# Second mixture of a three-stage kernel: the slices of an expert's first product packed into PSUM banks

## The chip, the cores and the metric

The kernel runs on one core of a Trainium2 chip. The metric is the device time of one execution in microseconds (us); less is better. TensorE (PE) multiplies into PSUM, VectorE (DVE) and ScalarE (ACT) read PSUM, GpSimd (POOL) issues gathers and scatters by index, SyncE (SP) issues the plain DMAs.

## What is computed

Attention, then two mixtures of experts in a row, all in float32. Cut to the second mixture, in which the change lies:

```python
def _moe2_ref(x, w_skip, w_gate, w1, w2):      # x [2304, 512], 8 experts, w1 [8, 512, 1024], w2 [8, 1024, 512]
    do_compute = x @ w_skip > 0
    xc = x[do_compute]
    e_idx = np.argmax(xc @ w_gate, axis=1)
    ...
    for e in range(E):
        mask = e_idx == e
        h = np.maximum(xc[mask] @ w1[e], 0.0)
        y[mask] = gate_w[mask, None] * (h @ w2[e])
    out[do_compute] = xc + y
```

Each token that is not skipped goes to one expert: a first product (512 to 1024 columns), relu, a second product (1024 to 512).

## The kernel before

The tokens of an expert are gathered in tiles of 128. `layer` (line 944) runs some tiles of one expert. Its first half makes the hidden values in KF = 8 slices f of 128 hidden columns: `mm1(x, f)` (line 873) takes a PSUM tile `h` of two banks from a pool of two (`ps_h`, so four of the eight banks), calls `products` (line 597) for the matmuls of this slice, and `hidden` (line 619) for its relu. After each slice it splits one eighth of the second weight (`w2split`, line 867) and lets queued side work advance by a step. Its second half, `mm2` (line 880), takes each tile's 8 x 3 matmuls of 512 columns over the slices in order.

The second product is made in three parts, from two halves of each operand: `hh` is the relu rounded to a shorter form (ACT, line 625), `hl` is the rest (DVE, line 626, reads the same PSUM slice and `hh`), `w2h` and `w2l` are the same of the weight (lines 854, 855). The three are `hh` by `w2h`, `hh` by `w2l`, `hl` by `w2h` (line 886). So a slice's PSUM bank is free again when DVE has made `hl`.

The first product has two forms. A layer of one tile is "native" (line 601): four float32 matmuls of 128 columns for each slice, two instructions each, 64 a layer, straight from the loaded weight. A layer of two tiles takes 12 split matmuls of 256 columns a slice (line 612). In both, a slice lies in the first of the two banks of its PSUM tile, and the second stays empty: one slice fills 128 or 256 of 512 columns.

The second mixture is ten layers, in this order: `p0a` and `p1a` (one tile each of the two experts that are known first), `p0b` (one tile), `p1b` (two), then `order[2]` and `order[3]` (two tiles each) and `order[4]` to `order[7]` (one each). Seven are native. Beside `p0a` and `p1a` runs the last part of the choice of experts, which those layers' loops advance (`aux2`, `tick`): `chain7` (line 1286) computes the gate of the tokens that the last expert of the first mixture wrote, with two small matmuls (`ranks`, lines 135 and 136), and scatters the result into `slots2`. `place_rest` (line 1395) then gathers the token lists (`meta`) and rows of `p0b` and `p1b` from it. Later layers gather the rows of the next layers in their first half: `r.load()` issues the gather of `meta`, and `load_ids` (line 567) turns it into indices on DVE (`tid`, line 568) behind the split of slice 5 or so, and issues the gather of the rows.

Nothing but the order of the program's text sets the order on each engine: each engine runs its instructions one after the other, and waits on semaphores of the others.

Of the kernel before, what the change touches and what calls it, by code (L numbers as in the profile page):

```python
# [8 lines left out]
F32 = mybir.dt.float32  # L9
F32R = mybir.dt.float32r  # L10
I32 = mybir.dt.int32
AF = mybir.ActivationFunctionType
OP = mybir.AluOpType
# [26 lines left out]
def attention_moe_moe(ctx, tc, qT, kT, vm, vr, tau, wgn, noise, w1a, w2a, wsg, w1b, w2b, out):  # L40
    nc = tc.nc
# [161 lines left out]
    def pool(stack, name, bufs, side="left", **kw):  # L203
        return stack.enter_context(tc.tile_pool(name=name, bufs=bufs, side=side, reuse_waits="tile", **kw))
# [392 lines left out]
    def products(x, f, ps):  # L597

        nn = x.n * 128
        parts = [(0, nn)] if nn <= 512 else [(0, nn // 2), (nn // 2, nn // 2)]  # L600
        if x.native:
            for kd in range(KD):
                nc.tensor.matmul(ps[:, 0, 0:nn], x.raw[0, f // 4][:, kd, (f % 4) * 128:(f % 4 + 1) * 128], x.xf[:, kd],
                                 start=(kd == 0), stop=(kd == KD - 1))
                if x.fine and kd == 1:
                    yield
        else:
            wh, wl = x.s1[f]
            for kd in range(KD):
                for j, (w, v) in enumerate(((wh, x.xh), (wh, x.xl), (wl, x.xh))):  # L610
                    for c, (a, m) in enumerate(parts):
                        nc.tensor.matmul(ps[:, c, 0:m], w[:, kd, :], v[:, kd, a:a + m],  # L612
                                         start=(kd == 0 and j == 0), stop=(kd == KD - 1 and j == 2))
                if kd < KD - 1:
                    yield
        m = parts[0][1]
        x.sums[f] = ps[:, 0:len(parts), 0:m]

    def hidden(x, f, hh, hl):
        src = x.sums.pop(f)  # L620
        m = src.shape[2]
        x.hid[f] = hh, hl
        dh = hh.rearrange("p (c m) -> p c m", m=m)
        dl = hl.rearrange("p (c m) -> p c m", m=m)
        nc.scalar.activation(dh, src, AF.Relu)  # L625
        nc.vector.scalar_tensor_tensor(dl, src, 0.0, dh.bitcast(F32), op0=OP.max, op1=OP.subtract)  # L626
# [132 lines left out]
    def early_mm1(k):  # L759
        if k < AHEAD:  # L760
            drain(products(e0a, k, ps_s.tile([128, 2, 512], F32, name="s")))
        if 0 < k <= AHEAD:
            hidden(e0a, k - 1, *(t[:, k - 1] for t in early["h"]))
# [6 lines left out]
    for u in range(NU):  # L770
        g, c, t, hh = UNITS[u]
# [37 lines left out]
        if (t, hh) == ((1, 1) if c == 0 else (4, 0)):  # L809
            k = (g, c)  # L810
# [37 lines left out]
    ps_h = pool(ctx, "ps_h", 2, space=PSUM)  # L848
# [24 lines left out]
    def mm1(x, f):  # L873
        if not x.hh:
            x.hh = [hp.tile([128, KF, SL1], F32R, name=nm) for nm in ("hh", "hl")] if x.kind == 1 else hid2
        ps = ps_h.tile([128, 2, 512], F32, name="h")
        yield from products(x, f, ps)
        hidden(x, f, *(t[:, f, 0:x.n * 128] for t in x.hh))

    def mm2(x, i):  # L880
        y = ps_y.tile([128, 512], F32, name="y")
        for f in range(KF):
            wh, wl = x.s2[f]
            hh, hl = x.hid[f]
            for j, (h, w) in enumerate(((hh, wh), (hh, wl), (hl, wh))):
                nc.tensor.matmul(y, h[:, i * 128:(i + 1) * 128], w, start=(f == 0 and j == 0),  # L886
                                 stop=(f == KF - 1 and j == 2))
            if (f % 2 or x.fine) and f < KF - 1:
                yield f % 2
        x.put(x, i, y)  # L890
# [53 lines left out]
    def layer(x, rate, W=None, nx=None, loads={}, eng=lambda f: nc.vector, rate2=0, rows=None):  # L944
# [4 lines left out]
        for f in range(KF):  # L949
            for _ in mm1(x, f) if f not in x.hid else ():  # L950
                if x.fine:
                    tick(rate)
            if x.native and f % 4 == 3:
                release(x, f // 4)
            for i in w2_at(x, f):
                w2split(x, i, eng(i))
                if i % 4 == 3:
                    release(x, 2 + i // 4)
            for k in loads:
                if loads[k] == f:  # L960
                    rawload(W, k)
            for i, r in enumerate(rows):
                if f == i:
                    r.load()
                if f == 5 + i:
                    load_ids(r)
            if x.ahead:
                w1split(W, f)
            tick(rate)
# [569 lines left out]
```

## Time and profile before

| | us |
|---|---|
| median of 3 runs (lowest, highest) | 1056.31 (1056.01, 1057.26) |
| the profiled execution's own time | 1054.67 |
| its span, first to last instruction | 1052.8 |
| PE busy in the span | 988.8 (94%) |
| DVE busy | 581.5 (55%) |
| ACT busy | 494.8 (47%) |

Attention takes the first 340 us or so, the first mixture lasts until about 850, the second one until the end. PE is the busiest engine over the whole and in nearly every slice of the span, so a question about the time is one about PE's gaps, where they lie and what ends them. Each matmul's duration overlaps that of the next one, so the distance between starts says how fast PE goes.

### The profile page before, as it was taken

To read this page: it belongs to the slowest core of one execution; us is meant where nothing else is said; L and a number is where in the kernel's file an instruction comes from. 1 tells how busy PE (TensorE), PEld (TensorE's weight loads), DVE (VectorE), ACT (ScalarE), POOL (GpSimd) and SP (SyncE) were. 2 spreads that over 40 slices of the span, in tenths; PEclk is the share of its full clock that TensorE was granted. 3 is DMA by queue.
4 is the path that set the end of the run, shared out by engine and by line. 5 is a ranking of instruction groups with operands and counts; after the bars stand their busy time and mean duration, and the time that the engine had idled before them with its cause. 6 is when DMAs were issued, how large, how long until landed. Compare 5 with 4: busy or idle time off the path is not lost. (4 is left out here: it accounts for less than half of the span.)

```text
span 1052.8 us, 16896 instructions
## 1 busy us (share of the span) xinstructions
PE 988.8 (94%) x6258; PEld 776.4 (74%) x6258; DVE 581.5 (55%) x1466; ACT 494.8 (47%) x939; POOL 294.0 (28%) x408
## 2 busy tenths in 40 slices
PE   6999999999988899999999999999999987899995
PEld 3555555555545797889888998989888776889894
DVE  6887888787785762453333242423323355667463
ACT  4766766666665542343333333333433232555352
POOL 3121143126205443230313122121322445122210
PEclk9999999999999899999999999999999999899998
DMA  7434454145400564463535445352453731666550
GB/s 149 107 88 129 126 148 89 50 109 146 157 28 1 200 181 91 126 190 89 151 66 144 109 134 118 93 153 66 105 169 80 271 116 69 241 209 209 187 210 17
DMA packets 54856, 134.76 MB, mean 128 GB/s; under 512 B 20043, under 2 KB 26475, under 8 KB 46064
## 3 DMA queue, kind: packets, MB, share of 16 engines
q1 hardware_dynamic: 41344, 107.17, 32.7%
q0 software_dynamic: 13424, 26.45, 11.0%
q8 instruction: 51, 0.84, 0.3%
q14 instruction: 37, 0.30, 0.1%
HBM read 112.64 MB, written 23.69 MB: 129 GB/s over the span
## 5 line engine op out<-in xcount | busy, mean ns | idle before, releaser
L626 DVE SCALAR_TENSOR_TENSOR hl<-h,hh 128x128 fp32r<-128x128 f32 (+3 forms) x157 | 80.1, 510 | 172.0 <-ACT hh L625 154.4
L886 PE MATMUL y<-w2h,hh 128*128 128x512 f32 x418 | 171.1, 409 | 1.3 <-ACT w2h L854 1.3
L625 ACT ACTIVATE hh<-h 128x128 fp32r<-128x128 f32 (+3 forms) x157 | 71.4, 455 | 200.5 <-PE h L612 147.8
L886 PE MATMUL y<-w2h,hl 128*128 128x512 f32 x418 | 164.7, 394 | 0.0
L886 PE MATMUL y<-w2l,hh 128*128 128x512 f32 x418 | 163.9, 392 | 0.2 <-DVE w2l L855 0.2
L612 PE MATMUL h<-xh,w1h 128*128 128x320 f32 (+2 forms) x596 | 154.3, 311 | 5.9 <-DVE hl L626 3.2
L612 PE MATMUL h<-xl,w1h 128*128 128x320 f32 (+2 forms) x596 | 152.2, 308 | 1.5 <-DVE xl L595 1.5
L612 PE MATMUL h<-xh,w1l 128*128 128x320 f32 (+2 forms) x596 | 151.6, 307 | 0.3 <-POOL w1l L855 0.3
L299 DVE TENSOR_REDUCE nm<-s 128x1 f32<-128x576 f32 x144 | 108.6, 754 | 44.5 <-PE s L291 43.5
L291 PE MATMUL s<-kr,qr 64*128 64x288 f32 (+1 forms) x640 | 111.9, 458 | 9.2 <-DVE kr L274 5.4
L301 ACT ACTIVATE e<-s,nm 128x576 f32<-128x576 f32 x144 | 106.3, 738 | 21.8 <-DVE nm L299 14.2
L612 PEld LDWEIGHTS h<-xh,w1h 128*128 128x128 f32 x596 | 105.1, 190 | 8.4 <-DVE hl L626 3.6
L612 PEld LDWEIGHTS h<-xl,w1h 128*128 128x128 f32 x596 | 105.4, 190 | 2.7 <-DVE xl L595 2.6
L612 PEld LDWEIGHTS h<-xh,w1l 128*128 128x128 f32 x596 | 105.4, 190 | 0.5 <-POOL w1l L855 0.5
L330 DVE SCALAR_TENSOR_TENSOR P<-s,th,e 128x576 f32<-128x576 f32 x128 | 103.4, 807 | 3.8
L342 ACT ACTIVATE pt<-tp 128x512 f32<-128x512 f32 x128 | 76.4, 597 | 60.4 <-PE tp L340 53.1
L895 POOL DMA_INDIRECT out_dram<-yo,tid x35 | 55.3, 1580 | 167.0 <-ACT yo L894 85.5
L340 PEld LDWEIGHTS tp<-ident,P 128*128 128x128 f32 x512 | 54.2, 141 | 55.9 <-issue 13.9
L886 PEld LDWEIGHTS y<-w2h,hl 128*128 128x128 f32 x418 | 79.0, 189 | 17.7
L886 PEld LDWEIGHTS y<-w2h,hh 128*128 128x128 f32 x418 | 79.3, 190 | 16.3 <-ACT w2h L854 1.7
L886 PEld LDWEIGHTS y<-w2l,hh 128*128 128x128 f32 x418 | 79.4, 190 | 14.7 <-DVE w2l L855 0.5
L340 PE MATMUL tp<-ident,P 128*128 128x128 f32 x512 | 84.8, 289 | 3.2 <-DVE xl L595 1.5
(269 smaller groups left out, 1434.1 us busy)
## 6 DMA issues: line engine op xcount, KB each, us to landing
rw<-in_w1a_dram SPq DMA_DIRECT2D x18, 1024.0 KB
rw<-in_w2a_dram SPq DMA_DIRECT2D x18, 1024.0 KB
qr<-in_qT_dram SPq DMA_DIRECT2D x30, 288.0 KB
rw<-in_w1b_dram SPq DMA_DIRECT2D x8, 1024.0 KB
rw<-in_w2b_dram SPq DMA_DIRECT2D x8, 1024.0 KB
kr<-in_kT_dram SPq DMA_DIRECT2D x96, 72.0 KB
out_dram<-zx SPq DMA_DIRECT2D x9, 512.0 KB
x<-xr SPq DMA_DIRECT2D x18, 256.0 KB
```

The lines of the kernel that those rows point to most:

```text
L291: nc.tensor.matmul(s[o, i, 0:SH], qr[r, h, t * 128:min((t + 1) * 128, S)], kr[r, h if t < 4 else 2 * h], start=True, stop=True)
L299: nc.vector.tensor_reduce(nm, s, axis=AX.XY, op=OP.max, negate=True)
L301: nc.scalar.activation(e, s, AF.Exp, bias=nm)
L330: nc.vector.scalar_tensor_tensor(o.rearrange("p (a b) -> p a b", a=2), s, th, e, op0=OP.is_ge, op1=OP.mult, accum_out=a)
L340: nc.tensor.transpose(ps[:, kt], P[:, c0 + kt * 128:c0 + (kt + 1) * 128], ident)
L342: nc.scalar.activation(ch["pt"][:, :, hh, (t % 2) * 128:(t % 2 + 1) * 128], ps, AF.Copy)
L612: nc.tensor.matmul(ps[:, c, 0:m], w[:, kd, :], v[:, kd, a:a + m], start=(kd == 0 and j == 0), stop=(kd == KD - 1 and j == 2))
L625: nc.scalar.activation(dh, src, AF.Relu)
L626: nc.vector.scalar_tensor_tensor(dl, src, 0.0, dh.bitcast(F32), op0=OP.max, op1=OP.subtract)
L886: nc.tensor.matmul(y, h[:, i * 128:(i + 1) * 128], w, start=(f == 0 and j == 0), stop=(f == KF - 1 and j == 2))
L895: nc.gpsimd.indirect_dma_start(out=x2[:, :], out_offset=bass.IndirectOffsetOnAxis(ap=tid, axis=0), in_=yo, in_offset=None, compute_op=OP.a ...
```

## The change

`mm1` of the second mixture goes through a new function, `packed`. A PSUM tile of two banks now holds several slices side by side: 512 // w in each bank, w being the columns of the layer's tiles. In a native layer (w = 128) one tile holds all eight slices, four in each bank; with two tiles (w = 256) it holds four slices, two in each bank, and a layer takes two PSUM tiles. The relu and the `hl` subtraction are issued once for each bank, behind the last slice in it, over 512 columns. `products` gets the place to write to instead of a tile.

```diff
@@ products @@
         if x.native:
             for kd in range(KD):
-                nc.tensor.matmul(ps[:, 0, 0:nn], x.raw[0, f // 4][:, kd, (f % 4) * 128:(f % 4 + 1) * 128], x.xf[:, kd],
+                nc.tensor.matmul(ps[:, 0:nn], x.raw[0, f // 4][:, kd, (f % 4) * 128:(f % 4 + 1) * 128], x.xf[:, kd],
                                  start=(kd == 0), stop=(kd == KD - 1))
...
-                        nc.tensor.matmul(ps[:, c, 0:m], w[:, kd, :], v[:, kd, a:a + m],
+                        nc.tensor.matmul(ps[:, c, 0:m] if len(ps.shape) > 2 else ps, w[:, kd, :], v[:, kd, a:a + m],
                                          start=(kd == 0 and j == 0), stop=(kd == KD - 1 and j == 2))
                 if kd < KD - 1:
                     yield
-        m = parts[0][1]
-        x.sums[f] = ps[:, 0:len(parts), 0:m]
+        if x.kind == 1:
+            x.sums[f] = ps[:, 0:len(parts), 0:parts[0][1]]
@@ mm1 @@
             x.hh = [hp.tile([128, KF, SL1], F32R, name=nm) for nm in ("hh", "hl")] if x.kind == 1 else hid2
+        if x.kind == 2:
+            yield from packed(x, f)
+            return
         ps = ps_h.tile([128, 2, 512], F32, name="h")
         yield from products(x, f, ps)
         hidden(x, f, *(t[:, f, 0:x.n * 128] for t in x.hh))
+
+    def packed(x, f):
+
+        w = x.n * 128
+        per = 512 // w
+        bank, k = divmod(f % (2 * per), per)
+        if f % (2 * per) == 0:
+            x.ps = ps_h.tile([128, 2, 512], F32, name="h")
+        yield from products(x, f, x.ps[:, bank, k * w:(k + 1) * w])
+        if k == per - 1:
+            src = x.ps[:, bank].rearrange("p (f m) -> p f m", m=w)
+            hh, hl = (t[:, f + 1 - per:f + 1, 0:w] for t in x.hh)
+            for j in range(per):
+                x.hid[f + 1 - per + j] = hh[:, j], hl[:, j]
+            nc.scalar.activation(hh, src, AF.Relu)
+            nc.vector.scalar_tensor_tensor(hl, src, 0.0, hh.bitcast(F32), op0=OP.max, op1=OP.subtract)
```

On PE, POOL and SP the instructions and their order are the same as before. ACT and DVE each issue 80 instructions for the ten layers' relu and `hl` before, and 26 now. Two places on DVE show how their order moves. The first is the end of the first half of `p0a`, where `chain7` begins: `w2l` is a split of the second weight, `ok` to `mask` are the gate's steps. Before:

```order
L626 SCALAR_TENSOR_TENSOR hl<-h,hh 128x128
L855 TENSOR_TENSOR w2l<-rw_8822,w2h 128x512
L1288 TENSOR_SCALAR ok_9144<-meta 128x5
...
L114 TENSOR_REDUCE fkc<-foc 128x5
L626 SCALAR_TENSOR_TENSOR hl<-h,hh 128x128
L855 TENSOR_TENSOR w2l<-rw_8822,w2h 128x512
L116 TENSOR_TENSOR foc<-foc,fkc 128x40
L1188 TENSOR_TENSOR ex<-lz_8037,fmc 128x40
L1192 TENSOR_TENSOR mask_9167<-foc,do 128x40
```

And now:

```order
L855 TENSOR_TENSOR w2l<-rw_8820,w2h 128x512 x2
L897 SCALAR_TENSOR_TENSOR hl<-h,hh 128x4x128
L855 TENSOR_TENSOR w2l<-rw_8820,w2h 128x512
L855 TENSOR_TENSOR w2l<-rw_8822,w2h 128x512 x3
L1307 TENSOR_SCALAR ok_9125<-meta 128x5
...
L114 TENSOR_REDUCE fkc<-foc 128x5
L897 SCALAR_TENSOR_TENSOR hl<-h,hh 128x4x128
L855 TENSOR_TENSOR w2l<-rw_8822,w2h 128x512
L116 TENSOR_TENSOR foc<-foc,fkc 128x40
```

The `hl` ahead of the gate's step in line 116 was that of slice 7, and is now that of slices 4 to 7.

The second place is the end of the first half of `order[5]`, where the index cast of a later layer's rows (`tid`, line 568) stands. Before:

```order
L626 SCALAR_TENSOR_TENSOR hl<-h,hh 128x128
L855 TENSOR_TENSOR w2l<-xl,w2h 128x512
L568 CAST tid<-meta 128x1
L626 SCALAR_TENSOR_TENSOR hl<-h,hh 128x128
L855 TENSOR_TENSOR w2l<-xl,w2h 128x512
L626 SCALAR_TENSOR_TENSOR hl<-h,hh 128x128
L855 TENSOR_TENSOR w2l<-xl,w2h 128x512
```

And now:

```order
L897 SCALAR_TENSOR_TENSOR hl<-h,hh 128x4x128
L855 TENSOR_TENSOR w2l<-xh,w2h 128x512
L855 TENSOR_TENSOR w2l<-xl,w2h 128x512 x2
L568 CAST tid<-meta 128x1
L855 TENSOR_TENSOR w2l<-xl,w2h 128x512
L897 SCALAR_TENSOR_TENSOR hl<-h,hh 128x4x128
L855 TENSOR_TENSOR w2l<-xl,w2h 128x512
```

The `hl` of slices 4 and 5 stood ahead of the cast, and now stands behind it with those of 6 and 7.

## Rows read from the trace of the kernel before

**Rows 1.** The page's first part: busy us, share of the span, instructions.
```profile
PE 988.8 (94%) x6258; PEld 776.4 (74%) x6258; DVE 581.5 (55%) x1466; ACT 494.8 (47%) x939; POOL 294.0 (28%) x408
```
**Rows 2.** A window: length; busy PE, PEld, DVE, ACT, POOL; PE's clock, DMA share, GB/s.
```profile
880.00:900.00 20.00, 13.71 (x73) 11.58 (x72) 7.79 (x28) 5.26 (x13) 8.67 (x14) 0.87 0.27 96
```
**Rows 3.** PE's waits, 854 to 1045 us: waited for, us, times, longest.
```profile
PE xt L584 <- DMA xt<-out_dram,tid: 3.9, 1, 3.9
PE rk L135 <- DVE mask L1192: 2.7, 1, 2.7
PE h L603 <- DVE hl L626: 1.7, 2, 1.3
PE h L612 <- DVE xl L595: 1.3, 1, 1.3
...
PE h L612 <- DVE hl L626: 0.5, 1, 0.5
```
**Rows 4.** Groups by form from 780 us on: count, busy us, mean ns, idle before.
```profile
L626 DVE SCALAR_TENSOR_TENSOR hl<-h,hh 128x128 fp32r<-128x128 f32 x56 | 15.9, 284 | 14.0 <-ACT hh L625 13.6 <-issue 0.4
L625 ACT ACTIVATE hh<-h 128x128 fp32r<-128x128 f32 x56 | 15.6, 278 | 47.7 <-PE h L603 42.9 <-PE y L886 2.8 <-issue 0.5
...
L588 ACT ACTIVATE xf<-xt 128x512 f32<-128x512 f32 x7 | 4.2, 595 | 13.9 <-PE xt L584 13.9
L595 DVE TENSOR_TENSOR xl<-xt,xh 128x512 fp32r<-128x512 f32 x6 | 4.1, 684 | 7.5 <-ACT xh L594 7.5
```
**Rows 5.** PE in time, first product of order[4]: start, length, engine, line, work.
```profile
986.61 4.02 PE L603 MATMUL h<-xf,rx 128*128 128x128 f32 x32
...
994.30 0.48 PE L886 MATMUL y<-w2h,hh 128*128 128x512 f32 x1
```
**Rows 6.** PE in time, the same of order[7], the last layer.
```profile
1027.73 7.89 PE L603 MATMUL h<-xf,rw 128*128 128x128 f32 x64
1035.38 0.48 PE L886 MATMUL y<-w2h,hh 128*128 128x512 f32 x1
```
**Rows 7.** PE in time, cut to the first two slices of order[7].
```profile
1027.73 1.95 PE L603 MATMUL h<-xf,rw 128*128 128x128 f32 x16
```
**Rows 8.** ACT in time: relu of slices 6 and 7 of p0a; idle before, releaser.
```profile
863.46 0.28 ACT L625 ACTIVATE hh<-h 128x128 fp32r<-128x128 f32 x1 [0.70 <-PE h L603]
...
867.07 0.28 ACT L625 ACTIVATE hh<-h 128x128 fp32r<-128x128 f32 x1 [2.81 <-PE y L886]
```
**Rows 9.** DVE in time: p0a's slice 7 and the gate's mask behind it.
```profile
867.38 0.29 DVE L626 SCALAR_TENSOR_TENSOR hl<-h,hh 128x128 fp32r<-128x128 f32 x1 [1.30 <-ACT hh L625]
...
868.73 0.20 DVE L1192 TENSOR_TENSOR mask<-foc,do 128x40 f32<-128x40 f32 x1
```
**Rows 10.** PE in time: p0a's slice 7, its second product, p0b's first product.
```profile
862.62 1.16 PE L603 MATMUL h<-xf,rw 128*128 128x128 f32 x8 [0.17 <-issue]
...
871.26 0.63 PE L886 MATMUL y<-w2h,hh 128*128 128x512 f32 x1
...
896.91 10.16 PE L603 MATMUL h<-xf,rw 128*128 128x128 f32 x64 [0.75 <-ACT xf L588]
```
**Rows 11.** POOL in time: a scatter of p0a's rows, gather of p0b's rows.
```profile
876.74 0.98 POOL L169 DMA_INDIRECT out_dram<-yo,tid  x1 [1.34 <-DVE yo L900]
...
888.98 1.02 POOL L177 DMA_INDIRECT xt<-out_dram,tid  x1 [0.21 <-issue]
```
**Rows 12.** POOL in time: rows of order[3]; a later layer's token list, during order[5].
```profile
951.47 1.47 POOL L177 DMA_INDIRECT xa<-out_dram,tid  x1 [5.88 <-issue]
...
1002.90 0.98 POOL L177 DMA_INDIRECT meta<-slots,rows  x1 [0.31 <-issue]
```
**Rows 13.** PE in time: the transposes that read the rows of order[3].
```profile
955.77 0.60 PE L584 MATMUL xt<-ident,xa 128*128 128x128 f32 x4
```
**Rows 14.** DVE in time: the index cast during order[5].
```profile
1010.28 0.15 DVE L568 CAST tid<-meta 128x1 int32<-128x1 f32 x1 [2.47 <-DMA meta<-slots,rows]
```
**Rows 15.** PE in time: first product of order[5].
```profile
1000.33 7.93 PE L603 MATMUL h<-xf,rw 128*128 128x128 f32 x64
```

## The prediction

> **What bounds the kernel now.** I began with the page: PE is busy for 988.8 of 1052.8 us [rows 1], DVE and ACT for about half. The change removes 54 instructions each from ACT and DVE and none from PE, so it can only pay where PE waits for these two. The windows of the second mixture say where PE has gaps: from 880 to 900 us it is busy for 13.71 of 20 us, and its mean granted clock is 0.87 [rows 2]. The waits of PE from `p0a` to the end are few and short [rows 3]: 3.9 us for the gathered rows of `p0b`, 2.7 us for the gate's mask, 1.7 us in native first products for `hl`, which is the wait for a free PSUM slot, 1.3 us for `xl`, 0.5 us for `hl` in a split first product. In the last layers PE shows as busy throughout, which hides small waits, since a matmul's duration overlaps the next one. So I read starts instead. The last layer's first product starts at 1027.73 and its second at 1035.38: 7.65 us for 64 instructions [rows 6]. Its first 16 last 1.95 us with a tail of 0.275 (their median duration), so 0.1117 us lies between two starts, and 64 would take 7.15 [rows 7]. PE loses 0.5 us there. `order[4]` takes 7.69, from 986.61 to 994.30 [rows 5].
>
> **The change, part by part.** The sum is made against the profiled execution, 1054.67 us of its own time; the median of the runs is 1056.31, and I put the result on that by the difference.
>
> *Work of ACT and DVE.* A relu of 128 columns takes 278 ns, an `hl` 284 [rows 4]. For 512 columns from PSUM the nearest rows are `xf` with 595 on ACT and `xl` with 684 on DVE [rows 4]. A native layer's eight pairs took 2.2 and 2.3 us and will take 1.2 and 1.4. By itself this is worth nothing, since PE's matmuls cover it.
>
> *Slots, last four layers.* Before, slice f waited until `hl` of slice f-2 was made, behind a split of `w2l` on DVE. Now a native layer has one PSUM tile for all eight slices and waits for none of its own `hl`. The bounds are nothing and 7.69 - 7.15, the whole loss. I take the whole, since four empty slices per bank leave nothing else to wait for: two layers like [rows 5] (the other is `order[5]`) and two like [rows 6], 0.54, 0.54, 0.50 and 0.50: -2.1 us.
>
> *A new wait, order[5].* The second bank's `hl` now stands behind the cast of `tid`, which ends a wait for a gather at 1010.28 [rows 14], 9.95 us after this layer's start at 1000.33 [rows 15]; the gather itself was issued at 1002.90 [rows 12]. Behind the cast come one `w2l` split and the new `hl`, about 0.7 us each, so `hl` is ready 11.4 us after the start. PE now ends its first product 7.15 us after the start, then runs 14 matmuls of the second at 0.227 us (the spacing of starts there) and four transposes, 0.36, and needs `hl` at about 10.8. It waits 0.6: +0.6 us, with bounds of 0 (the gather lands earlier) and 2. Behind it on DVE stands only the last `w2l`, which PE needs 2 us later.
>
> *The other bank ends.* In the other native layers the last relu starts when the last slice is done, ends 0.6 us later, and `hl` 0.7 after that: 1.4 us with the handovers. PE works for 12 matmuls x 0.227 = 2.7 us on slices 0 to 3 before it comes to slice 4. That hides it, with 1.3 us to spare. With two tiles the last bank holds slices 6 and 7 only, and 4.1 us hide it.
>
> This is where the Trainium skill speaks against the change. "Perfetto Trace Analysis", section "Matmuls", wants independent matmul groups to rotate through different PSUM banks, so that emptying one overlaps the next group; here four groups follow each other in one bank, and by that rule the emptying of every second bank, 1.3 us, would come on top in ten layers. The rows above say that the second product covers it, and the sum goes by them.
>
> *order[2].* PE waits 0.5 us there for `hl` of a slice two back [rows 3]. The two-tile layers get a new PSUM tile for slice 4, so that wait goes: -0.5 us.
>
> *Start of p1b.* PE waits 1.3 us for `xl` [rows 3], while DVE works without a gap through the splits of `p0b` and `p1b`. DVE saves 8 x 0.284 - 2 x 0.684 = 0.9 us in `p0b`. Bounds 0 and 1.3; I take -0.8, as ACT's `xh` comes close behind.
>
> *The chain around p0a.* PE waits 2.7 us for the mask [rows 3], and what follows hangs on it: the second product of `p0a`, its scatter on POOL at 876.74 [rows 11], behind that in POOL's order the last scatters of `chain7`, then the token list, then the gather of `p0b`'s rows at 888.98 [rows 11], for which PE waits the 3.9 us. Now the mask comes behind `hl` of slices 4 to 7 on DVE. Slice 7's matmuls run from 862.62 for 1.16 us [rows 10], but its relu starts at 867.07 only [rows 8], and `hl` at 867.38 [rows 9]: PE's signal came 3.3 us after the last matmul, in a stretch in which POOL issued one scatter after another. Slice 6's signal was 1 us late, its relu at 863.46 [rows 8]. What makes PE's signals late the trace doesn't tell. Without slot waits PE ends slice 7 about 1 us earlier, at 862.8, when slice 6 ended before. DVE, with seven small `hl` fewer and one of 0.7 more, reaches the place at about 864.5. If the signal is late by 1 us, as slice 6's was, relu ends at 864.4 and DVE waits for nothing: `hl` 0.7, `w2l` 0.6, and the mask is there at about 866.1 in place of 868.73 [rows 9], 2.6 us earlier. PE's gap of 2.7 us all but goes, and with it the half clock behind it: from 871.26 on a matmul of `y` takes 0.63 us in place of 0.39 [rows 10], 8 starts 0.43 us apart in place of 0.23, 1.7 us in all. So the chain moves by up to -4.3. If the signal comes at 867.07 as before, relu is 0.3 and `hl` 0.4 us longer, and the chain moves by +0.7. I take the nearest row, slice 6's, so -4.3, and give 1.3 of it back: `p1a` ends its work earlier by more than the rows of `p0b` come, PE's gap before them grows from 3.9 to about 6, and the half clock after it (64 instructions of `p0b` take 10.16 us against 7.4 [rows 10, 7]) may last longer. That makes -3.0.
>
> The sum: -2.1 + 0.6 - 0.5 - 0.8 - 3.0 = -5.8, that is 1048.9 on the profiled execution's own time and 1050.5 on the median.
>
> **Rivals.** *The chain doesn't move.* Slice 7's signal is as late as before. Then the terms give -2.1 + 0.6 - 0.5 - 0.8 + 0.7 = -2.1: 1054.2. For it speaks that the scatters run in the same place; against it that slice 7 now ends where slice 6 did.
>
> *The change frees only idle engines.* The small waits of PE are there for another reason than the slots, and the chain stands: 1056.3, no change. For it: PE is busy throughout by the windows. Against it: the 1.7 us in native first products are put down to `hl` [rows 3].
>
> *Slower: the rows come too late.* In a two-tile layer the cast of `tid` stands behind an `hl` and a split of a whole bank, about 0.45 us later against PE. The rows of `order[3]` were asked for at 951.47 [rows 12] and read at 955.77 [rows 13] without a wait, 4.3 us. `p0b`'s took from 888.98 to PE's start after the wait of 3.9, some 6.1. If those of `order[2]` and `order[3]` take as long (4.8 and 4.3 us were there), PE waits 1.7 and 2.2 us, and if the clock falls after each as after the mask's 2.7, that costs 1.7 twice. With the chain not moved: -2.1 + 3.9 + 3.4 = +5.2, 1061.5. It decides at a latency of about 4.3 us.
>
> *Slower: a bank is emptied in the open.* The page's rule as a mechanism: 10 layers x 1.3 us, and the slots' gains remain: 13 - 2.1 - 0.5 - 0.8 = +9.6, 1065.9. It would need DVE to come to the last `hl` 1.3 us later than the rows have it, in all layers.
>
> **How the numbers follow.** About 0.2%, 2.1 us, can be told from no change. Chances: forecast 0.58 (its own range 1046.5 to 1053), chain not moved 0.22 (at the border: 0.13 faster, 0.09 same), idle engines only 0.12, rows too late 0.05, bank in the open 0.03. So faster 0.71, same 0.21, slower 0.08. The low end has the full chain and the whole wait at `p1b`: -2.1 - 0.5 - 1.3 - 4.3 and a spread of the runs of 1 us, 1047; the high end is the unmoved chain and the same spread, 1055.5. I take 1046.5 to 1055.5, which leaves out a fifth.
>
> **What would show it.** Right: 7.15 us from first to second product in the last two layers; no wait for `hl` in L603; the mask before 867 us, no half clock near 871, the rows of `p0b` read near 891 to 892. A wait of PE for `hl` in the second product of `order[5]` of about 0.6. Wrong: the relu of the second bank of `p0a` near 867 again; waits for rows in `order[2]` or `order[3]`; PE waiting for `hl` in the second products of `order[6]` and `order[7]`.

## The result, and the profile after

The changed kernel took 1063.6 us (median of 8 runs, 1062.21 to 1066.59), the kernel before 1054.05 beside it (8 runs, 1049.09 to 1057.26): a ratio of 1.0104 as recorded, 95% interval 1.0083 to 1.0125 (the two medians alone give 1.0091). It is slower by 1%. The forecast was faster, and its range ended at 1055.5. The profiled execution took 1066.08 us with a span of 1064.2.

The page's first part, of the changed kernel (it answers to [rows 1]):

```profile
PE 986.8 (93%) x6258; PEld 774.5 (73%) x6258; DVE 571.7 (54%) x1412; ACT 485.6 (46%) x885; POOL 296.4 (28%) x408
```

DVE and ACT have the 54 instructions and some 10 us less, as the change says. PE has the same number of instructions and as much work, in a span that is 11 us longer: the time went into PE's gaps. Two windows of the second mixture say where (columns as in [rows 2]):

```profile
880.00:900.00 20.00, 16.22 (x93) 14.50 (x92) 8.55 (x22) 5.35 (x11) 9.62 (x12) 0.86 0.33 104
...
1020.00:1040.00 20.00, 18.53 (x126) 16.69 (x125) 8.75 (x14) 7.36 (x14) 2.09 (x3) 1.00 0.25 97
```

Around the gather of `p0b`'s rows PE is busier than before, 16.22 in place of 13.71 us. In the last layers 1.47 us of 20 are gone. The kernel before was busy throughout there:

```profile
1020.00:1040.00 20.00, 20.00 (x128) 17.85 (x129) 11.18 (x24) 9.32 (x23) 1.07 (x2) 1.00 0.04 13
```

PE's waits from 854 us on name the cause (they answer to [rows 3]):

```profile
PE h L603 <- DVE hl L897: 12.9, 7, 4.2
PE h L612 <- DVE hl L897: 8.8, 6, 1.5
PE xt L584 <- DMA xt<-out_dram,tid: 1.6, 1, 1.6
...
PE h L612 <- DVE xl L595: 0.8, 1, 0.8
```

Thirteen waits of a first product for `hl`: one in each of the seven native layers, two in each of the three two-tile layers, that is one for each PSUM tile of the change, 21.7 us in all. Before, [rows 3] had 2.2 us of such waits. Where the wait falls is seen in the last layer, first PE in time, then ACT, then DVE:

```profile
1037.99 3.73 PE L603 MATMUL h<-xf,rw 128*128 128x128 f32 x32
1043.19 3.84 PE L603 MATMUL h<-xf,rw 128*128 128x128 f32 x32 [1.47 <-DVE hl L897]
1046.79 0.49 PE L905 MATMUL y<-w2h,hh 128*128 128x512 f32 x1
```

```profile
1041.82 0.60 ACT L896 ACTIVATE hh<-h 128x512 fp32r<-128x512 f32 x1 [5.55 <-PE h L603]
```

```profile
1042.45 0.69 DVE L897 SCALAR_TENSOR_TENSOR hl<-h,hh 128x512 fp32r<-128x512 f32 x1 [1.71 <-ACT hh L896]
```

Slices 0 to 3 (32 instructions) fill the first bank and end at 1037.99 + 3.73 = 1041.72. The relu of that bank follows at 1041.82, its `hl` at 1042.45, which ends at 1043.14. Slice 4 starts at 1043.19. It writes into the second bank, which nobody reads; it waits all the same until the first bank is emptied. From first to second product the layer takes 1046.79 - 1037.99 = 8.80 us, against 7.65 in [rows 6].

A table of stages, in us, of three kernels; the third is the first experiment below. The first stage starts with PE's start of `p0a`'s first product, and each ends with the start that its row names, where the next one begins (so the time of `order[2]` stands in the row of `order[3]`).

| the stage ends with | before | change | a tile for each bank |
|---|---|---|---|
| PE reading the rows of `p0b` | 41.60 | 38.96 | 36.92 |
| first product of `p1b` | 19.14 | 19.12 | 18.03 |
| of `order[2]` | 25.07 | 29.23 | 25.31 |
| of `order[3]` | 24.26 | 27.05 | 23.55 |
| of `order[4]` | 23.09 | 26.60 | 23.09 |
| second product of `order[7]` (four layers) | 48.77 | 53.33 | 46.32 |
| sum | 181.93 | 194.29 | 173.22 |

The change loses 12.36 us here and starts the second mixture 0.95 us earlier (852.50 against 853.45): 11.41, which is 1066.08 - 1054.67.

### The profile page after: what moved, and what is told of

Read it like the earlier page. It is cut to its first block, busy times and chain, and to the rows that moved or that the text cites. A ratio compares the mean times of both kernels' runs of the same rounds, so it can differ in the third digit from the quotient of the medians.

```text
span 1064.2 us, 16808 instructions
## 1 busy us (share of the span) xinstructions
PE 986.8 (93%) x6258; PEld 774.5 (73%) x6258; DVE 571.7 (54%) x1412; ACT 485.6 (46%) x885; POOL 296.4 (28%) x408
## 5 line engine op out<-in xcount | busy, mean ns | idle before, releaser
L626 DVE SCALAR_TENSOR_TENSOR hl<-h,hh 128x640 fp32r<-128x640 f32 (+2 forms) x77 | 54.0, 701 | 149.7 <-ACT hh L625 134.5
L625 ACT ACTIVATE hh<-h 128x640 fp32r<-128x640 f32 (+2 forms) x77 | 46.6, 606 | 134.3 <-PE h L612 129.3
L905 PEld LDWEIGHTS y<-w2l,hh 128*128 128x128 f32 x418 | 78.8, 189 | 14.5 <-DVE w2l L855 0.5
```

## The experiments

Twelve runs. Ratios are to the kernel before, run beside each; an unchanged copy of it gave 0.9984 (0.9966 to 1.0003) and 0.9997 (0.9975 to 1.0020), so some 0.2% is what such a ratio can be off by.

**A PSUM tile for each bank.** Relu and `hl` stay once per bank. Only the place of the second bank's slices changes: the first bank of a new tile.

```diff
-        bank, k = divmod(f % (2 * per), per)
-        if f % (2 * per) == 0:
+        k = f % per
+        if k == 0:
             x.ps = ps_h.tile([128, 2, 512], F32, name="h")
-        yield from products(x, f, x.ps[:, bank, k * w:(k + 1) * w])
+        yield from products(x, f, x.ps[:, 0, k * w:(k + 1) * w])
...
-            src = x.ps[:, bank].rearrange("p (f m) -> p f m", m=w)
+            src = x.ps[:, 0, 0:per * w].rearrange("p (f m) -> p f m", m=w)
```

> As the change, but every bank's group of slices gets a PSUM tile of its own (the first bank of it); relu and hl are once per bank as in the change. Theory A (one order per tile: a write into a PSUM tile waits for every earlier read of that tile, in whichever bank): the 13 waits of 1.5 us of PE between the first and the second bank go; from first to second product in the last four layers 7.15 us; the earlier chain around p0a stays; 6 us under the kernel before, ratio 0.9945 (0.992 to 0.997). Theory B (a relu and an hl over 512 columns are too late for PE whichever tile they are read from): the waits move to the next group or to the second product, the time stays within 2 us of the change, ratio 1.009.

Measured: 1043.73 beside 1052.02 us, ratio 0.992 (0.9895 to 0.9945). All 13 waits in first products are gone; one of 1.5 us for an `hl` is left, in `p1a`'s second product. PE's waits from 850 us on:

```profile
PE xt L584 <- DMA xt<-out_dram,tid: 4.4, 1, 4.4
PE h L612 <- DVE xl L595: 1.6, 1, 1.6
PE y L905 <- DVE hl L897: 1.5, 1, 1.5
...
PE rk L135 <- DVE mask L1211: 0.5, 1, 0.5
```

and the last layer, PE in time, then the relu and `hl` of its first four slices on ACT and DVE:

```profile
1015.73 7.30 PE L603 MATMUL h<-xf,rw 128*128 128x128 f32 x64
1022.79 0.48 PE L905 MATMUL y<-w2h,hh 128*128 128x512 f32 x1
```

```profile
1019.50 0.60 ACT L896 ACTIVATE hh<-h 128x512 fp32r<-128x512 f32 x1 [5.48 <-PE h L603]
```

```profile
1020.13 0.69 DVE L897 SCALAR_TENSOR_TENSOR hl<-h,hh 128x512 fp32r<-128x512 f32 x1 [1.65 <-ACT hh L896]
```

PE's 64 instructions run on while the other two read. They take 7.06 us, against 8.80 with the change and 7.65 before. The instructions of PE, ACT and DVE and their order are those of the change; only the tile differs, and that is worth 194.29 - 173.22 = 21.1 us in the table: 13 waits at 8.80 - 7.06 = 1.74 us would be 22.6 (`p1a`'s is longer, but hidden in part by the wait for `p0b`'s rows). Theory A holds, B falls: the same relu and `hl` over 512 columns cost the last layer's first product nothing when PE may go on into another tile. The list of the program's instructions, with the semaphores on which each waits, shows it too. Slices 4 to 7 of `order[6]` in the change, and below with a tile for each bank (this list has a float32 matmul once, the trace shows it as two instructions):

```
L603 MATMUL h<-xf,rx_8996 128x128 [waits DMAHW6_49,DVE_49]
L603 MATMUL h<-xf,rx_8996 128x128 x15

L603 MATMUL h<-xf,rx_8996 128x128 [waits DMAHW6_49,PE_49]
L603 MATMUL h<-xf,rx_8996 128x128 x15
```

In the change the first matmul of the second bank has a wait on DVE, and the 15 behind it have none; with a tile for each bank it waits for PE's own earlier work in place of DVE. The wait for a DMA is the same in both. So the wait is an order that the program carries, not one that PE takes of itself.

**Two slices of one tile in two banks, nothing packed.**

```diff
+        if f % 2 == 0:
+            x.ps = ps_h.tile([128, 2, 512], F32, name="h")
+        src = x.ps[:, f % 2, 0:w]
+        yield from products(x, f, src)
+        hh, hl = x.hid[f] = tuple(t[:, f, 0:w] for t in x.hh)
+        nc.scalar.activation(hh, src, AF.Relu)
+        nc.vector.scalar_tensor_tensor(hl, src, 0.0, hh.bitcast(F32), op0=OP.max, op1=OP.subtract)
```

> Relu and hl per slice as before, but one PSUM tile for two slices, the even one in its first bank, the odd one in its second, in all ten layers. Nothing is packed into a bank. Theory A: each odd slice waits for relu and hl of the slice ahead of it, 40 waits of 0.8 to 1.4 us: 25 to 50 us over before, ratio 1.024 to 1.047. If only accesses to one and the same bank are ordered (theory C): no such wait, and four slots in place of two: 2 us under before, ratio 0.998.

Measured: 1083.6 us, ratio 1.0301 (1.0268 to 1.0334). PE's waits:

```profile
PE h L603 <- DVE hl L892: 22.0, 23, 2.4
PE h L612 <- DVE hl L892: 10.9, 11, 1.0
```

and the last slice of the last layer, on PE and then DVE:

```profile
1064.17 1.16 PE L603 MATMUL h<-xf,rw 128*128 128x128 f32 x8 [0.92 <-DVE hl L892]
```

```profile
1063.83 0.28 DVE L892 SCALAR_TENSOR_TENSOR hl<-h,hh 128x128 fp32r<-128x128 f32 x1
```

Slice 7 waits for the `hl` of slice 6, made from the other bank. No bank is shared here and no view is rearranged, so theory C falls. A write into a PSUM tile of this program waits for the earlier reads of that tile, in whichever bank: 34 waits of about 1 us for `hl`, at 40 odd slices (the profile puts most of the others to a split of `w2l` or names nothing).

**Where the gain of a tile for each bank lies.** Groups in `p0a` and `p1a` alone, in the other eight layers alone, and in `p0a` alone; the edit is `per = 512 // w if x.fine else 1`, its reverse, and `if x is p0a`.

> Groups of four slices, a tile for each, in p0a and p1a alone; all other layers one slice per tile and relu and hl per slice, as before. If the chain around p0a is what moved in the change (mask earlier, no half clock behind it, rows of p0b earlier): rows of p0b read 3 to 4 us earlier than before, the layers behind it as long as before, time 3.5 us under before, ratio 0.9967 (0.995 to 0.999). If that was chance of PE's late signals: mask near 868 again, ratio 1.000.

Measured: 0.9966 (0.9951 to 0.9981), as expected; 36.63 us from `p0a`'s first product to `p0b`'s rows.

> Groups with a tile for each in the eight layers behind p0a and p1a, which stay as before. Theory A with the terms of the prediction: -2.1 for the slots of the last four layers, +0.6 for the wait in order[5], -0.5 in order[2], -0.8 at p1b: 2.8 us under before, ratio 0.9973 (0.995 to 0.999). If only the chain counts: 1.000. Theory B: above 1.005.

Measured: 0.9964 (0.9946 to 0.9982), a little more than expected, though its trace gives less: 1.0 us from `p0a` to the end. There the last four layers take 2.4 us less than before, `order[2]` 0.7 and the stage of `p0b` 0.6, but the first stage 1.2 more, and `p1b` 1.5 more. In it `p0a` is as before, and the relu of its slices 6 and 7 comes late again (ACT in time, slice 6 and then slice 7; slice 7's matmuls end at 859.30):

```profile
859.70 0.28 ACT L896 ACTIVATE hh<-h 128x128 fp32r<-128x128 f32 x1 [1.42 <-PE h L603]
862.65 0.28 ACT L896 ACTIVATE hh<-h 128x128 fp32r<-128x128 f32 x1 [2.15 <-PE y L905]
```

> Groups of four slices in p0a alone, a tile for each. If the chain runs through p0a's last hl and the mask only: the rows of p0b are read as early as with p0a and p1a grouped (36.6 us behind the start of p0a's first product against 41.6 before), ratio 0.9967 as there. If p1a's slot waits take part: 2 to 3 us of that are lost.

Measured: 1.0008 (0.9990 to 1.0026), no gain where 0.9967 was expected, although the rows of `p0b` are read 35.22 us behind the start of `p0a`. The kernel before ran at 1039.89 us beside it, not at 1052.02 as beside the earlier ones. That raised the question of the last runs.

**Two slices in a group** (`per = 2`), in the same set of runs:

> Groups of two slices in every layer, a PSUM tile and one relu and hl for each group (in the native layers four groups, in the two-tile layers as with a tile for each bank). If the gain of a tile for each bank comes from the room that a slot gives PE (the hl that it waits for is a whole group back), two slices are room enough in the native layers: first to second product of the last four layers 7.1 to 7.2 us, ratio within 0.002 of 0.992. If it comes from having only two pairs of relu and hl in a layer, the small waits are there again: 7.4 us or more in the last layers. Where PE's signal for the last slices of p0a is late again (3 us, as with one slice per group), the mask is late and 3 to 4 us of the gain are lost: ratio 0.995 to 0.996.

Measured: 0.9975 (0.9958 to 0.9992), beside the same 1039.89 us; the ratio missed the expected 0.992, for the reason that the last runs look for. The last layer is as expected:

```profile
1009.10 7.30 PE L603 MATMUL h<-xf,rw 128*128 128x128 f32 x64
```

The same 7.30 as with four in a group. So the gain in the first products is the room of a slot: PE waits for the `hl` of a group back, and two slices are enough. The number of relus and `hl`s has no part in that.

**Does the late signal belong to the kernel?** The kernel before again, three of the versions beside it, and the kernel before a third time.

> The kernel before, unchanged, for its trace beside the three others. Open is why groups in p0a gained 0.34% beside one set of runs of the kernel before (median 1052.0 us) and nothing beside another (1039.9 us). Theory D (late signals differ from one set of runs to another): where the kernel before runs at about 1040 us, the relu of p0a's slice 7 follows its last matmul within 0.5 us, and from the start of p0a's first product to p0b's rows it takes about 37 us in place of 41.6; where it runs at about 1052, the relu is 3.3 us late and it takes 41 to 42 us. Theory E (the late signal belongs to the one relu per slice): 3.3 us late in either. Ratio 1.000.

> The kernel before once more, for the other half of theory D, since in the earlier set it ran at 1052 us with the late signal. If it runs at about 1040 us here: theory D has the relu of p0a's slice 7 within 0.5 us behind its last matmul and about 37 us from the start of p0a's first product to p0b's rows; theory E has it 3.3 us late. If it runs at about 1052 again, late by 3.3 us under both, and the question stays open.

It ran at 1052.25 us the one time and at 1040.22 the other. `p0a`'s slice 7 on PE, and its relu on ACT, at 1052:

```profile
863.35 1.16 PE L603 MATMUL h<-xf,rw 128*128 128x128 f32 x8 [0.15 <-issue]
```

```profile
867.86 0.28 ACT L625 ACTIVATE hh<-h 128x128 fp32r<-128x128 f32 x1 [2.85 <-PE y L886]
```

and at 1040:

```profile
848.06 6.66 PE L603 MATMUL h<-xf,rw 128*128 128x128 f32 x52
```

```profile
854.75 0.28 ACT L625 ACTIVATE hh<-h 128x128 fp32r<-128x128 f32 x1 [0.23 <-PE h L603]
```

The relu comes 3.35 us behind the last matmul (863.35 + 1.16 = 864.51) in the one and 0.03 in the other (848.06 + 6.66 = 854.72). The first stage takes 40.76 and 35.73 us, `order[2]` to `order[3]` 24.26 and 23.55. Theory D holds in these two traces, and E falls: the same program has the late signal in one set of runs and not in the other. But the late signal at `p0a` is only a part of the 12 us between the two medians. The two traces are 14.5 us apart (spans 1050.8 and 1036.3), and 9.5 of these lie ahead of `p0a`'s first product, which starts at 854.19 in the one and at 844.68 in the other, in work that no version changes. Nor does the chip alone decide: by the record the sets at 1052.02 and at 1039.89 us both ran on chip 8. In the traces of all kernels with groups in `p0a`, in either condition, the relu of its last group is there within 0.3 us.

> As tile_per_bank_p0a_p1a. Theory D: 0.9966 beside a kernel before with a late signal, 0.999 to 1.001 beside one without. Theory E: 0.9966 in either.

Measured: 0.9967 (0.9947 to 0.9988) beside a kernel before with the late signal, as D and E both have it.

> As tile_per_bank. Theory D: ratio 0.992 beside a kernel before with a late signal, 0.995 to 0.997 beside one without (only the slots and p0b are left: -2.5 in the last four layers, -0.7 in order[2], -1.1 in p0b). Theory E: 0.992 in either.

Measured: 0.9946 (0.9925 to 0.9966) beside a kernel before with the late signal, where D and E both had 0.992. The gain is smaller than theirs, though the interval overlaps with that of the first run. Of what its trace has more than the first one's, 1.2 us lie in the first stage and 1.5 in `p1b`, where a half clock follows PE's wait for `xl` (columns as in [rows 2]; the first one had a mean of 1.00 at that place, so the half clock that the next expectation speaks of is not in its trace):

```profile
908.00:911.00 3.00, 2.43 (x11) 2.44 (x12) 1.72 (x3) 0.00 (x0) 2.19 (x3) 0.58 1.01 423
```

**That wait taken away.** `p1b`'s transposes and splits moved to the front of `p0b`'s second product:

```diff
-            soon += [((i + 0.5) / nx.n, xt, (nx, i)) for i in range(nx.n)]
+            soon += [((i + 0.5) / nx.n * (0.3 if x.kind == 2 and nx.n > x.n else 1), xt, (nx, i)) for i in range(nx.n)]
```

> A tile for each bank as before, and the transposes and splits (xh, xl) of p1b's two tiles move from the middle and the end of p0b's second product to its first quarter and its middle. If PE's 1.6 us for xl and 0.7 for xh at the start of p1b, and the half clock behind them, are only due to that order, they go: 2 to 3 us under the run with a tile for each bank, ratio 0.989 to 0.990. If DVE is the limit there (its splits of w1 come late instead), the wait moves to w1l in the first slices of p1b and nothing is won: 0.992.

Measured: 0.9949 (0.9930 to 0.9968) beside the kernel before at 1039.89 us; two slices in a group, of the same set, had 0.9975. The expected 0.989 to 0.990 was for a kernel before at 1052 us; `p1b` takes 23.71 us in place of 25.31. PE with a tile for each bank, and then with the move:

```profile
904.52 0.38 PE L612 MATMUL h<-xh,w1h 128*128 128x256 f32 x1 [0.69 <-ACT xh L594]
906.49 0.39 PE L612 MATMUL h<-xl,w1h 128*128 128x256 f32 x1 [1.59 <-DVE xl L595]
```

```profile
900.76 0.28 PE L612 MATMUL h<-xh,w1h 128*128 128x256 f32 x1
900.87 0.28 PE L612 MATMUL h<-xl,w1h 128*128 128x256 f32 x1
```

> As tile_per_bank_early_rows; beside tile_per_bank_2 in the same set of runs: p1b takes 23.7 us in place of 25.3 and p0b's part no longer, so 1.5 to 3 us, 0.0015 to 0.003 of the ratio, below it.

Measured: 0.9916 (0.9893 to 0.9939), 0.003 below the run beside it; the two intervals overlap, but the traces have 3.4 us less from `p0b`'s rows to the end of `p1b`. Both waits are gone, and none for `w1l` took their place. In the second of these runs PE meets a new one of 0.9 us, for the rows of `order[2]`, since it comes to them sooner. This version was the fastest in both sets that it ran in, and its ratio to the kernel before is below 1 in both.

## Why the prediction was wrong

**The step that failed** stands in the part on slots: "Now a native layer has one PSUM tile for all eight slices and waits for none of its own `hl`". It waits for the `hl` of its first bank, because both banks are one tile. The same holds in the sentence on `order[2]`, where "the two-tile layers get a new PSUM tile for slice 4, so that wait goes": within each tile, a new one comes between slices 1 and 2. The price of emptying a bank was right, "1.4 us with the handovers"; 1.47 us of wait and 1.74 with the start behind it were measured. It was put at the end of the second bank, where the second product covers it. It fell behind the first bank, where nothing does, 13 times.

**Slots, last four layers**, -2.1: +4.6 in the change (53.33 - 48.77), and -2.45 with a tile for each bank (46.32 - 48.77). The mechanism was right for a layout that the change is not. The 1.7 us of [rows 3], which the prediction held against the rival of idle engines, lie in `p1a`, though, and not in these layers:

```profile
881.08 1.16 PE L603 MATMUL h<-xf,xl 128*128 128x128 f32 x8 [0.37 <-DVE hl L626]
883.55 2.15 PE L603 MATMUL h<-xf,xl 128*128 128x128 f32 x16 [1.31 <-DVE hl L626]
```

The distance of starts is what bore the term out. `p0b` gains from the slots as well, which the sum left out: 1.1 us in the second row of the table.

**The wait in order[5]**, +0.6: none in the change, where the first product is longer, and none in tile_per_bank, where the gather landed sooner. In tile_per_bank_2 the cast came 9.4 us behind the layer's start, nearly as late as in [rows 14], and PE's starts in `y` lost about 0.1 us there. The wait is possible; its size was at the low bound.

**order[2]**, -0.5: not seen in the change, which lost 2.8 there. With a tile for each bank -0.7; but the kernel before itself took 23.55 when its signals were not late, without that wait. So the wait came of a late signal, which a group covers, and is not there without one.

**Start of p1b**, -0.8: the wait for `xl` was 0.8 in the change, but 1.6 with a tile for each bank. When PE is faster through `p0b`, DVE comes no sooner; the wait is set by the order of DVE's work, as the last experiment shows.

**The chain around p0a**, -3.0: -2.64 in the change, in spite of a wait of 4.2 us between the banks of `p1a`, and -4.68 with a tile for each bank. On ACT, DVE and PE of the change (relu of slices 4 to 7, mask, the matmul behind it, and the rows of `p0b`):

```profile
863.66 0.60 ACT L896 ACTIVATE hh<-h 128x512 fp32r<-128x512 f32 x1 [2.58 <-PE h L603]
```

```profile
865.73 0.20 DVE L1211 TENSOR_TENSOR mask<-foc,do 128x40 f32<-128x40 f32 x1
```

```profile
866.08 0.39 PE L135 MATMUL rk<-mask,before 128*128 128x40 f32 x2
...
891.46 0.66 PE L584 MATMUL xt<-ident,xt 128*128 128x128 f32 x4 [1.56 <-DMA xt<-out_dram,tid]
```

The mask came 3.0 us earlier than in [rows 9] (2.0 counted from `p0a`'s start), PE's gap before it went, and the half clock behind it too (867.40 to 870.93 for the matmuls that took 870.40 to 875.51), and the rows were read at 891.46, in the forecast's "near 891 to 892". That is in part luck: PE ended slice 7 at 863.63 because of the wait between the banks, not at 862.8, and the signal was not 1 us late but 0.03, so the relu ended at 864.26 where the prediction had 864.4. Moreover the signal that had been late in [rows 8] is late in some runs of the kernel before only; in the others there is little to gain here (35.73 us in the kernel before, 35.22 with groups in `p0a`).

**The rivals.** "A bank is emptied in the open" had 3% and 1065.9 us, close to the result by chance, since it was for another place: the second bank, ten times, with DVE late. No second product waits for the second bank in the change. The rule behind it (the Trainium skill, "Perfetto Trace Analysis", section "Matmuls": rotate independent groups through banks) would not have told the change from its mended version either, as both put four groups into a bank and then go to another one; one loses 21 us to the other. What tells them apart is whether the next group lies in the same tile. The Trainium skill, "PSUM — Partial Sum Buffer", section "PSUM bank collisions raise a hardware error", wants two engines kept apart only where they touch one and the same bank; by that the 13 waits guard nothing. The trace agrees as far as it can: with a tile for each bank PE's matmuls run from 1015.73 to 1023.03 without a gap, in the second half into one bank while ACT and DVE read another from 1019.50 to 1020.82. "The rows come too late" did not occur: no wait for rows in `order[2]` or `order[3]`.

Without the 13 waits the forecast's sign and its two large terms hold: -5.8 forecast, -8.7 in the table and 0.992 and 0.9946 as ratios beside a kernel before with the late signal. The larger of the two, the chain, hangs on that signal.

## What to carry to other kernels

Two banks of one PSUM tile are one buffer to the program's ordering: let the next group of matmuls write into a new tile, not into the free half of the one that is being read. Before a packed layout is costed, read the semaphore waits of the changed program at the first write behind each read, and not only the order of its instructions; the wait on DVE stood there. And a saving that removes a late signal should be measured beside runs of the old kernel that have it and beside runs that don't.

## What was not expected of the hardware

PE's signal to ACT at the end of `p0a`'s first product was 3.3 us late in three traces with one relu per slice (the profiled kernel before, its first copy, and tile_per_bank_rest) and not late in the copy that ran at 1040 us; the other stages show it as well (`order[2]`, 12.40 against 11.68 us for its first product). POOL issued its scatters at that place in both conditions, so these alone don't cause it. Nor does the one relu per slice: two_slices_two_banks has it too, ran beside the kernel before at 1052 us, and its relu of slice 7 started at 864.43, 0.03 us behind the matmuls. The late signals are not a matter of the second mixture alone, as the 9.5 us ahead of it show. What makes the signal late, and why the kernels with groups were spared in every trace, stays open; no run was aimed at it.
